# First quad of heads prepared pair by pair, and the software queue's loads in a new order

## The chip, the cores and the metric

One core of one Trainium2 chip runs the whole kernel. The metric is the device time of one execution in microseconds (us); lower is better. Engines are named as in the profile: PE (matrix), PEld (its weight loads), DVE (vector), ACT (scalar), POOL (GpSimd, which also issues the software DMA queue), SP (which issues a hardware DMA queue).

## The reference, cut to what matters

```python
q, k, v: (8, 12, 448, 64)                 # batch, heads, sequence, head width
q_n, k_n = rmsnorm(q, g_q), rmsnorm(k, g_k)
attn = softmax(q_n @ k_n.T / sqrt(64))    # per head, 448 x 448
x = (attn @ v) -> (3584, 768)             # heads side by side again
a, b = x @ w1, x @ w2                     # 768 -> 1024, twice
out = (a * b @ w3) @ w_out                # 1024 -> 1024 -> 768, float32
```

## The kernel before, in words

**Tiling.** The 96 heads are taken in 24 *quads* of four, three quads to a batch. A quad's q and k lie in one buffer as `[128 partitions, q/k, pair x, 7, 64]`: pair x holds two heads, one on each half of the partitions. So the two *pairs* of a quad are x = 0 and x = 1. `w3 @ w_out` does not depend on x, so the kernel forms the product once (`w34s`) in the beginning, from `w3` (transposed on PE into `w3T`) and `w_out`; afterwards each batch costs two products with w1 and w2 (line 868, `xT` with `w1s`/`w2s`), a multiplication, and one product with `w34s`.

**What a quad passes through.** Loads of q and k (line 367); squares on ACT (`sq`, 464); their sums on DVE (`red`, `ssq`, 471); Ln and Exp on ACT for the root (`alpha`, 480 and 483); the multiplication on DVE into bf16 (`scale`, `qks`, 494); a transpose to `[head width, tokens]`, on PE for the first five quads (line 1123, `do_turn`, two turns of seven) and by DMA for the rest (561); copies out of PSUM into `qkT` (352 on ACT, 358 on DVE), where q is also multiplied by the product of the two weight rows (`g_col`); seven *scores* (line 679, four matmuls of 448 columns each), every one followed by an Exp of 128x896 on ACT (701); and then the product with v (*PV*, lines 745 and 766), for two quads at a time mostly. One score takes both pairs: its four matmuls are for u = 0 and u = 1 in each half, and u is the pair:

```python
    for c in range(2):
        ...
        for u in range(2):
            nc.tensor.matmul(
                ...
                lhsT=qkT[u * D : (u + 1) * D, 1, j, cols],
                rhs=qkT[u * D : (u + 1) * D, 0, :, cols],
```

**What sets the order.** The kernel is built by a planner: `Planner.run` walks through time with an estimate for each job (the numbers given to `add`), and writes each engine's instructions in the order in which that plan starts them. On the chip each engine then takes its own list. Constants such as `QUAD`, `HUNGRY`, `PACE`, `STOCK`, `LOW`, `SOON`, `QUIET`, `LATE`, `WARM_TO`, `AHEAD_W3` only move choices in this plan. PE's choices are in `pe_try`: an open PV, scores, *turns* (transposes of `qks` or of w3), and *passes*, a pass being four matmuls of line 868. Where the plan finds nothing for PE before `WARM_TO`, it puts in a filler matmul on zeros (line 1193); sixteen matmuls of 512 columns on zeros (line 1316) stand at the start.

**The loads.** The first quad comes over the two hardware queues, SP and ACT. All weights, v, and q and k of quads 1 to 5 go over the software queue, issued by POOL in the order of `POOL_ORDER`: `wN` is a piece of w3 (512 KB read, 256 KB written as bf16), `oN` a quarter of w_out, `aN` and `bN` thirds of w1 and w2, `qN` q and k of a quad, `vN` its v in four pieces. A pass for `w34s` needs the transposed piece of w3 and the quarter of w_out that it works on; four passes belong to each pair of one `w` and one `o`, 128 in all.

Of the kernel before, what the change touches and what calls it, by code (L numbers as in the profile page):

```python
# [20 lines left out]
SEM = 0.05  # L21
# [3 lines left out]
LAG = {"ACT": 0.11, "DVE": 0.09, "SP": 0.0, "POOL": 0.0}  # L25
AHEAD = {"SP": 2.0, "POOL": 1.6}
AFTER = 0.7
LATE = 0.3
BUSY = 75.0


# [14 lines left out]
class Planner:  # L46
# [11 lines left out]
    def add(self, *args, **kw):  # L58
        self.jobs.append(Job(*args, **kw))
# [136 lines left out]
def kernel(  # L196
# [40 lines left out]
    psum = ctx.enter_context(tc.tile_pool(name="ps", bufs=1, space=PSUM))  # L237

    N_PE_T = 5
    QUAD = 13.0  # L240
    WARM = 15
    WARM_TO = 13.0
    WARM_N = 256
    MAX_PAIRS = 2
    MARGIN = 0.25
    LOW = 2
    PV_BANKS = 6
    HOLD = 0
    SOON = 0
    STARVED = 4  # L250
    HUNGRY = 0.6
    ONE = 0
    PARTS = ((2, 4, 6, 8), (2, 4, 6, 8), (4, 8))
    EARLY_PAIRS = 3
    AHEAD_W3 = 4
    EARLY = 4
    STOCK = 14
    PACE = 1.7
    POOL_ORDER = (
        "o0 w0 w1 w2 o1 o2 o3 q1 v0 w3 w4 q2 w5 a0 v1 w6 w7 v2 a1 v3 q3 a2 b0 b1 q4 q5 b2".split()  # L260
    )
    ON_POOL = (1, 2, 3, 4, 5)
    IN_PARTS = (6, 7, 8)
    FIRST = 3.5
    THIN_FROM, THIN = 8, 2.5
    QUIET = 0.5

    w1s = const.tile([128, CM, DFF], BF, name="w1s")
    w2s = const.tile([128, CM, DFF], BF, name="w2s")
# [80 lines left out]
    def copy_on(engine, out, in_, by=None):  # L350
        if engine == "ACT":
            nc.scalar.activation(  # L352
                out=out, in_=in_, func=AF.Copy, scale=1.0 if by is None else by
            )
        elif by is not None:
            nc.vector.tensor_scalar(out=out, in0=in_, scalar1=by, scalar2=None, op0=MULT)
        else:
            nc.vector.tensor_copy(out=out, in_=in_)  # L358
# [93 lines left out]

    def plan_prep(i):
        s = st[i]
        pe = i < N_PE_T
# [43 lines left out]
        def by_g():  # L501
# [3 lines left out]
                in1=g_b.unsqueeze(1).broadcast_to([NP, 2 * NJ, D]), op=MULT,  # L505
            )

        alpha_at = [INF, INF]
        red_parts = [[], []]
        s["red_at"] = [INF, INF]  # L510
# [135 lines left out]
    def score_ready(t):  # L646
        n = next_score[0]
        if n >= NQ * NU:
            return False
        i, g = divmod(n, NU)  # L650
        if g == 0 and min(p_free(x, i) for x in range(4)) > t:
            return False
        stock = sum(p.name != "w" for p in waiting)
        if stock >= STOCK and t < last_score[0] + PACE:
            return False
        return max(qkT_at[i]) + SEM <= t

    def do_score(t, z):
        n = next_score[0]
# [57 lines left out]
    def pv_size(t):  # L717


        i = next_pv[0]  # L720
        if not pv_one(i, t):
            return 0
        if i + 1 >= NQ:
            return 1
        if pv_one(i + 1, t):
            return 2
        if next_score[0] >= (i + 2) * NU - SOON:
            return 0
        if i == 1:
            return 0  # L730
        stock = sum(p.name != "w" for p in waiting)
        return 1 if stock < LOW or all_of(w34_at, CF) > t else 0

# [376 lines left out]
            tiles = range(NT - 1) if odd else ()  # L1110
        waiting.extend(ffn2_pair(bp, t) for t in tiles)

    turns = [(i, w) for i in range(N_PE_T) for w in range(2)]
    w3_turns = list(range(CF))

    def do_turn(t, i, w, z):
        s = st[i]
        ps = ps_all[:, z, :].bitcast(BF)[:, 0 : NJ * NP].rearrange(
            "p (j s) -> p j s", j=NJ
        )  # L1120
        took = into("t") + NJ * 0.067
        for j in range(NJ):
            nc.tensor.transpose(  # L1123
                ps[:, j], s["qks"][:, w, j].rearrange("p x d -> p (x d)"), ident
            )
        bank_at[z] = INF
        at = t + took + 0.18
        s["sent"][w] = at

        def done(e):  # L1130
            bank_at[z] = e + SEM
            qkT_at[i][w] = e

        add(
            None, {"DVE": 0.53, "ACT": 0.83}, -950.0 + i,
            lambda e: copy_on(e, s["qkT"][:, w], ps, None if w else g_col),
            needs=[lambda: at, lambda: consts_at["g"]], done=done,
        )
        return took
# [28 lines left out]
    def any_turn(t, r, idle, n):  # L1168

        if not idle:  # L1170
            return None
        if turns:
            i, w = turns[0]
            if scaled_at[i][w] <= r:
                turns.pop(0)
                return do_turn(t, i, w, single(idle))
        ready = [fc for fc in w3_turns if w_at["w3"][fc] + SEM <= r]
        if ready and (len(ready) >= n or ready[-1] == CF - 1):
            if ready[0] - len(w34_at) < AHEAD_W3:
                return do_w3_turn(t, w3_turns.pop(0), single(idle))  # L1180
        return None

    def pe_step(t):

        took = pe_try(t, t - MARGIN)
        took = pe_try(t, t) if took is None else took
        if took is None and t < WARM_TO and idle_banks(t):
            return do_warm(single(idle_banks(t)))
        return took
# [108 lines left out]
    with tc.manual_schedule():  # L1298
        nc.vector.memset(warm_t, 0.0)
        nc.vector.memset(eps_t, 64e-6)  # L1300
        nc.vector.memset(ones, 1.0)
        nc.vector.memset(ones[HP:NP, 1], 0.0)
        nc.vector.memset(ones[0:HP, 2], 0.0)
        nc.vector.memset(ones_row, 1.0)
        for which in range(2):
            load_qk(0, which, nc.sync, 0, 1)
            load_qk(0, which, nc.scalar, 1, 2)
        nc.scalar.dma_start(out=g_row[:, 0], in_=g_q.unsqueeze(0))
        nc.scalar.dma_start(out=g_row[:, 1], in_=g_k.unsqueeze(0))
        nc.scalar.preload_act_table_set("natural_log_exp_and_others")  # L1310
        make_identity(nc, ident)
        for t_sb in v_bufs:
            nc.gpsimd.memset(t_sb[:, :, NF, :], 0.0)
        def warm(n):
            for _ in range(n):
                nc.tensor.matmul(  # L1316
                    out=ps_all[:, 7, :], lhsT=warm_t[:, 0:128], rhs=warm_t,
                    start=True, stop=True,
                )

        def g_product():
            nc.vector.scalar_tensor_tensor(
                out=gp_row,
                in0=g_row[:, 0].unsqueeze(1).broadcast_to([1, 2, D]),
                scalar=8.0,
                in1=g_row[:, 1].unsqueeze(1).broadcast_to([1, 2, D]),
                op0=MULT, op1=MULT,
            )
            nc.tensor.matmul(
                out=ps_all[:, 6, 0:D], lhsT=ones_row, rhs=gp_row[:, 0],  # L1330
                start=True, stop=True,
            )
            nc.tensor.matmul(
                out=ps_all[:, 6, D : D + 1],
                lhsT=gp_row.rearrange("a x d -> a (x d)"), rhs=ones_row[:, 0:1],
                start=True, stop=True,
            )
            warm(1)

        def spread():  # L1340
            nc.vector.tensor_copy(out=g_b, in_=ps_all[:, 6, 0:D])
            nc.vector.tensor_copy(out=g_col, in_=ps_all[:, 6, D : D + 1])

        warm(WARM)
        free.update(ACT=4.0, DVE=4.0, SP=4.0, POOL=2.3, PE=7.2)
        plan.now = plan.moved_to = 2.2
        plan.moving["SP"].append([2.3, FIRST, lambda t: None, 0.086])
        landed[0].update(q=4.5, k=5.4)
        bank_at[6] = INF
        add(  # L1350
            "DVE", 0.13, -13.0, g_product, needs=[lambda: 5.8], done=put(consts_at, "gp")
        )
        add(
            "DVE", 0.22, -11.0, spread, needs=[lambda: consts_at["gp"] + 0.6],
            done=lambda t: consts_at.update(g=t + SEM) or bank_at.__setitem__(6, t + SEM),
        )
        for i in range(3):
            plan_prep(i)

        seq = [0]  # L1360

        def weight(emit, moves, done):
            add("POOL", 0.6, -100.0 + seq[0], emit, done=done, moves=moves)

        for name in POOL_ORDER:
            what, x = name[0], int(name[1])
            seq[0] += 1
            if what == "o":
                weight(lambda x=x: load_wout(x), (1.95, 0.135), put(w_at["w_out"], x))
            elif what == "w":  # L1370
                weight(lambda x=x: load_w3(x), (1.27, 0.172), put(w_at["w3"], x))
            elif what == "v":
                plan_load_v(x, -100.0 + seq[0])
            elif what == "q":
                plan_load_qk(x, -100.0 + seq[0])
            else:
                dst, src, key = (w1s, moe_w1, "w1") if what == "a" else (w2s, moe_w2, "w2")
                weight(
                    lambda dst=dst, src=src, x=x: load_w12(dst, src, x), (2.7, 0.323),
                    put(w_at[key], x),  # L1380
                )
        waiting.extend(w34_pair(fc) for fc in range(CF))
        plan.run(pe_step, finished)
        if PLAN_OUT is not None:
            PLAN_OUT.append(dict(free))
# [28 lines left out]
```

## Time and profile before

| what | value |
|---|---|
| median of six runs | 353.68 us (352.86 to 354.38) |
| the profiled execution | 354.06 us, of which 352.2 us are the span from the first to the last instruction |
| granted PE clock over the span | 1.00 |
| busy: PE, ACT, DVE, POOL | 344.6, 262.0, 206.8, 76.8 us |
| DMA, mean over the span | 156 GB/s; 16.92 MB on the software queue |
| first score on PE, first Exp on ACT | 11.29 us, 11.72 us |

Times inside the span count from its start. A row of the timeline or of the chain of work gives start, duration, engine, line, output and input, and how many instructions are merged; a bracket is the idle time of the engine before it and what ended that.

### The profile page before, as it was taken

The numbers are of one execution on the slowest core, as the hardware profiler recorded it, in microseconds if no ns is written. First come the engines' busy times: TensorE is split into PE (matmuls) and PEld (weight loads), VectorE is DVE, ScalarE is ACT, GpSimd is POOL, SyncE is SP. The second block draws the span as 40 slices with busy tenths as digits, with TensorE's granted clock in tenths as the row PEclk, the third lists the DMA queues.
The fourth block names the chain that finished last, engine by engine and source line by source line (L and its number), as shares of the span: only waits on it lengthen the run. The fifth ranks groups of instructions, "written<-read, shape, count | busy, mean of one in ns | idle before, by whom it ended". The sixth has DMA issues, their size and how long they took to land.

```text
span 352.2 us, 16197 instructions
## 1 busy us (share of the span) xinstructions
PE 344.6 (98%) x7374; PEld 225.0 (64%) x7374; DVE 206.8 (59%) x293; ACT 262.0 (74%) x375; POOL 76.8 (22%) x134
## 2 busy tenths in 40 slices
PE   8999999999999999999999999999999999999995
PEld 4767656657655766469856575566665656666674
DVE  5379378997989297895869758566643321222200
ACT  4779979989899989797989898777886942222122
POOL 8376720304212223113131031330130000000000
PEclk9999999999999999999999999999999999999999
DMA  8999999599999999987999979852590013100054
GB/s 194 238 284 192 239 314 238 95 199 235 195 201 187 196 173 227 193 172 176 207 218 166 225 97 254 220 70 40 115 177 6 4 47 105 37 2 2 5 164 153
DMA packets 68488, 55.11 MB, mean 156 GB/s; under 512 B 45060, under 2 KB 62372, under 8 KB 68420
## 3 DMA queue, kind: packets, MB, share of 16 engines
q1 hardware_dynamic: 49440, 35.33, 45.1%
q0 software_dynamic: 18048, 16.92, 27.4%
q10 hardware_dynamic: 932, 1.84, 1.4%
q8 instruction: 57, 0.93, 1.1%
q14 instruction: 11, 0.09, 0.1%
HBM read 46.66 MB, written 11.01 MB: 164 GB/s over the span
## 4 chain that ended last, share of the span: by engine, by line
PE 88%; ACT 5%; DVE 3%; DMA 2%; issue 1%; DVEq 0%; POOLq 0%
PE ps_all L868 62%; PE ps_all L766 11%; PE ps_all L679 9%; ACT P L701 3%; DMA qkT<-qks 2%; PE ps_all L745 2%; PE ps_all L1316 2%; DVE qks L494 1%; PE ps_all L1123 1%; PE ps_all L1064 1%; ACT sq L464 1%; PE ps_all L1145 1%; DVE ssq L471 1%; PE ps_all L1193 1%; DVE xT L808 1%
## 5 line engine op out<-in xcount | busy, mean ns | idle before, releaser
L701 ACT ACTIVATE P<-ps_all 128x896 bf16<-128x896 f32 x114 | 99.4, 922 | 12.3 <-PE ps_all L679 12.0
L407 POOL DMA_DIRECT2D v_sb<-in_v_dram x96 | 57.1, 616 | 177.3 <-PE ps_all L679 89.2
L868 PE MATMUL ps_all<-xT,w2s 64*64 64x448 bf16 x1536 | 88.9, 349 | 0.6 <-DVE xT L808 0.4
L868 PE MATMUL ps_all<-xT,w1s 64*64 64x448 bf16 x1536 | 89.0, 349 | 0.1
L868 PE MATMUL ps_all<-w34s,abT 64*64 64x384 bf16 x1728 | 80.5, 323 | 0.0
L352 ACT ACTIVATE half<-ps_all 128x896 bf16<-128x896 f32 (+1 forms) x38 | 33.3, 877 | 49.4 <-PE ps_all L868 49.3
L949 DVE TENSOR_TENSOR abT<-ps_all,half 128x896 bf16<-128x896 f32 x32 | 34.9, 1089 | 54.4 <-PE ps_all L868 54.3
L868 PEld LDWEIGHTS <-abT 64*64 64x64 bf16 x1728 | 55.1, 107 | 17.3 <-issue 0.7
L868 PEld LDWEIGHTS <-w2s 64*64 64x64 bf16 x1536 | 48.4, 107 | 25.7 <-issue 1.4
L868 PEld LDWEIGHTS <-w1s 64*64 64x64 bf16 x1536 | 47.4, 107 | 25.5 <-POOLq L852 0.9
L679 PE MATMUL ps_all<-qkT 64*64 64x448 bf16 x672 | 62.1, 352 | 0.8 <-ACT Pr L701 0.4
L471 DVE TENSOR_REDUCE ssq<-sq 128x14 f32<-128x896 f32 (+1 forms) x50 | 51.3, 1042 | 18.9 <-ACT sq L464 18.9
L494 DVE TENSOR_TENSOR qks<-qk_sb,al 128x448 bf16<-128x448 f32 x96 | 55.9, 618 | 1.4 <-ACT al L483 1.4
L464 ACT ACTIVATE sq<-qk_sb 128x896 f32<-128x896 f32 (+1 forms) x50 | 45.4, 922 | 1.7 <-DVE ssq L471 1.1
L808 DVE TENSOR_TENSOR xT<-ps_all,r 128x448 bf16<-128x448 f32 x48 | 27.7, 619 | 13.2 <-ACT r L789 10.3
L679 PEld LDWEIGHTS <-qkT 64*64 64x64 bf16 x672 | 23.1, 106 | 14.2 <-issue 4.8
L868 PE MATMUL ps_all<-w_outs,w3T 64*64 64x384 bf16 x512 | 25.1, 323 | 0.7 <-DVE w3T L358 0.5
L701 ACT ACTIVATE w_outs<-ps_all 128x896 bf16<-128x896 f32 x24 | 21.6, 913 | 5.2 <-PE ps_all L679 4.8
L766 PE MATMUL ps_all<-P,v_sb 128*32 128x448 bf16 x456 | 25.2, 353 | 0.0
L766 PEld LDWEIGHTS <-v_sb 128*32 128x32 bf16 x592 | 15.9, 97 | 12.5 <-issue 0.5
L701 ACT ACTIVATE Pr<-ps_all 128x896 bf16<-128x896 f32 x24 | 22.1, 921 | 0.1
L358 DVE COPY half<-ps_all 128x768 f32<-128x768 f32 x13 | 12.4, 955 | 13.9 <-PE ps_all L868 13.2
(65 smaller groups left out, 213.1 us busy)
## 6 DMA issues: line engine op xcount, KB each, us to landing
out_dram<-half SPq DMA_DIRECT2D x48, 192.0 KB, 3.6
qk_sb<-in_q_dram SPq DMA_DIRECT2D x15, 448.0 KB, 5.0
qk_sb<-in_k_dram SPq DMA_DIRECT2D x15, 448.0 KB, 5.6
v_sb<-in_v_dram POOLq DMA_DIRECT2D x48, 64.0 KB, 3.8
v_sb<-in_v_dram POOLq DMA_DIRECT2D x48, 48.0 KB, 3.8
qk_sb<-in_q_dram POOLq DMA_DIRECT2D x5, 448.0 KB, 12.0
qk_sb<-in_k_dram POOLq DMA_DIRECT2D x5, 448.0 KB, 11.8
w3s<-in_moe_w_dram POOLq DMA_DIRECT2D x8, 256.0 KB, 6.7
```

Of the source, the lines that this page charges most:

```text
L352: nc.scalar.activation(out=out, in_=in_, func=AF.Copy, scale=1.0 if by is None else by)
L358: nc.vector.tensor_copy(out=out, in_=in_)
L407: nc.gpsimd.dma_start(out=v_bufs[i % 4][p0 : p0 + HP, g::2, 0 : j1 - j0].rearrange("p h j d -> p h (j d)"), in_=src[:, g::2, j0:j1].rearra ...
L464: nc.scalar.activation(out=s["sq", t][:, x0:x1], in_=src[:, t, x0:x1], func=AF.Square)
L471: nc.vector.tensor_reduce(out=s["ssq"][:, t, x0:x1], in_=s["sq", t][:, x0:x1], axis=AX, op=ADD)
L494: nc.vector.tensor_tensor(out=s["qks"][:, t, :, x], in0=src[:, t, x], in1=s["alpha"][:, t, x].unsqueeze(2).broadcast_to([NP, NJ, D]), op=MULT,
L679: nc.tensor.matmul(out=sc[HP * c : HP * c + HP, u, 0:S].rearrange("p (j s) -> p j s", j=NJ), lhsT=qkT[u * D : (u + 1) * D, 1, j, cols], rh ...
L701: lambda: nc.scalar.activation(out=dst, in_=sc[:, :, 0:S], func=AF.Exp),
L766: nc.tensor.matmul(out=ps_all[hd * HALF : (hd + 1) * HALF, z, 0:S], lhsT=value_weights(i, hd, j, kind), rhs=s["P"][:, hd, j, :] if j < NF ...
L808: lambda: nc.vector.tensor_tensor(out=xT[b][:, 2 * m + kind - 1, :], in0=ps, in1=s["r"], op=MULT),
L868: mm = nc.tensor.matmul(out=ps_all[64 * h : 64 * h + 64, p.bank + z, 0 : p.n], lhsT=lhsT[64 * r : 64 * r + 64, 64 * h : 64 * h + 64], rhs= ...
L949: nc.vector.tensor_tensor(out=abT[bp][:, f0 : f0 + 2, odd * S : (odd + 1) * S], in0=ps_all[:, z : z + 2, 0:S], in1=a_sb[b, f0], op=MULT,)
```

## The change

The first quad no longer goes through `prep`'s general path. `prep_by_pair` takes pair 0 of q and k, then pair 1: squares, sums, one Ln and one Exp for q and k of a pair together, multiplications. `do_pair_turn` transposes 64 columns of `qks` at a time, so a pair of q or k is one turn of seven transposes (four turns instead of two), and copies it to its 64 partitions of `qkT`. The first loads go accordingly: q on SP, k on ACT, pair 0 first on both. `score_ready` lets the plan take the first three scores once pair 0 is there; `do_score` itself is the same. `POOL_ORDER` starts with w0 in place of o0, moves q1 and v0 ahead of w2 and o3, and puts v1, v2 and v3 behind w7, with b0 and a1 before. A number of planner constants change.

```diff
-LATE = 0.3
+LATE = 0.401
-    QUAD = 13.0
+    QUAD = 12.269
-    WARM_TO = 13.0
+    WARM_TO = 12.754
-    MARGIN = 0.25
-    LOW = 2
+    MARGINS = (0.25, 0.0)
+    SINGLES = None
+    BY_PAIR = True
+    LOW = 3
-    SOON = 0
+    SOON = 2
-    HUNGRY = 0.6
+    HUNGRY = 0.609
-    AHEAD_W3 = 4
+    AHEAD_W3 = 6
-    PACE = 1.7
+    PACE = 1.73
     POOL_ORDER = (
-        "o0 w0 w1 w2 o1 o2 o3 q1 v0 w3 w4 q2 w5 a0 v1 w6 w7 v2 a1 v3 q3 a2 b0 b1 q4 q5 b2".split()
+        "w0 o0 o1 w1 o2 q1 v0 w2 o3 w3 w4 q2 w5 a0 w6 b0 a1 w7 v1 v2 v3 q3 b1 a2 q4 q5 b2".split()
     )
-    QUIET = 0.5
+    QUIET = 0.424
+    PAIR_AT = (4.28, 5.36)
...
+    def prep_by_pair(s, src, sq, red, scale):
...
+            for t in range(2):
+                add(
+                    "ACT", 0.40, -14.0 + 2 * x + t * 0.1, lambda t=t: sq(t, x, x + 1),
+                    needs=[lambda: PAIR_AT[x]], done=put(hold[t], "at"),
+                )
+                add(
+                    "DVE", 0.53, -13.0 + 2 * x + t * 0.1, lambda t=t: red(t, x, x + 1),
+                    needs=[lambda t=t: hold[t].get("at", INF) + SEM], done=reduced,
+                )
+                add(
+                    "DVE", 0.54, -16.0 + 2 * x + t * 0.1, lambda t=t: scale(t, x),
+                    needs=[lambda: al.get("at", INF) + SEM], done=done(t),
+                )
+            add(
+                "ACT", 0.45, -16.0 + x, lambda: alpha(x),
+                needs=[lambda: all_of(got, 2) + SEM], done=put(al, "at"),
+            )
...
-        return max(qkT_at[i]) + SEM <= t
+        at = max(pair_at[0]) if BY_PAIR and n < NF else max(qkT_at[i])
+        return at + SEM <= t
...
+    def do_pair_turn(t, x, w, z):
+        s = st[0]
+        rows = slice(D * x, D * x + D)
+        ps = ps_all[:, z, :].bitcast(BF)[rows, 0 : NJ * NP].rearrange(
+            "p (j s) -> p j s", j=NJ
+        )
+        took = into("u") + NJ * 0.067
+        for j in range(NJ):
+            nc.tensor.transpose(ps[:, j], s["qks"][:, w, j, x], ident)
...
+        add(
+            None, {"DVE": 0.53, "ACT": 0.87}, -950.0,
+            lambda e: copy_on(e, s["qkT"][rows, w], ps, None if w else g_col[rows]),
+            needs=[lambda: at, lambda: consts_at["g"]], done=done,
+        )
...
-            load_qk(0, which, nc.sync, 0, 1)
-            load_qk(0, which, nc.scalar, 1, 2)
+            if BY_PAIR:
+                load_qk(0, 0, nc.sync, which, which + 1)
+                load_qk(0, 1, nc.scalar, which, which + 1)
```

## The prediction

> **What bounds it now.** I read the page first, then the timelines of the first 30 us, engine by engine, then the chain of waits, then the windows.
>
> ```profile
> span 352.2 us, 16197 instructions
> PE 344.6 (98%) x7374; PEld 225.0 (64%) x7374; DVE 206.8 (59%) x293; ACT 262.0 (74%) x375; POOL 76.8 (22%) x134
> ```
>
> PE is the bound: 98% busy, and the chain of waits lies on it for 88%. The change takes no useful matmul away. So the end moves by what changes in PE's idle and filler time. The next rows show the start, from the timelines of ACT, DVE and PE.
>
> ```profile
> 4.09 2.23 ACT L464 ACTIVATE sq<-qk_sb 128x448 f32<-128x448 f32 x4 [0.28 <-DMA qk_sb<-in_q_dram]
> ...
> 7.21 2.21 DVE L494 TENSOR_TENSOR qks<-qk_sb,al 128x448 bf16<-128x448 f32 x4
> ...
> 9.01 1.01 ACT L352 ACTIVATE qkT<-ps_all,g_col 128x896 bf16<-128x896 bf16 x1 [1.34 <-PE ps_all L1123]
> ...
> 10.16 0.62 DVE L358 COPY qkT<-ps_all 128x896 bf16<-128x896 bf16 x1 [0.74 <-PE ps_all L1123]
> ...
> 11.72 5.10 ACT L701 ACTIVATE P<-ps_all 128x896 bf16<-128x896 f32 x6 [1.71 <-PE ps_all L679]
> 12.11 0.45 PEld L1145 LDWEIGHTS <-w3s 128*128 128x128 bf16 x8 [0.30 <-DMA w3s<-in_moe_w_dram]
> ```
>
> The chain to the first Exp (11.72) is squares, sums, roots, four multiplications, transposes and copies; PE runs fillers, its first score is at 11.29. The Exps then follow every 0.83 us, and the seventh (16.71) ends at 17.63. The last row shows PE waiting for a piece of w3. POOL's timeline tells when loads land, because from its ninth on, a load waits for the one eight before it:
>
> ```profile
> 10.97 0.60 POOL L407 DMA_DIRECT2D v_sb<-in_v_dram  x1 [0.38 <-DMA w3s<-in_moe_w_dram]
> 12.23 0.59 POOL L407 DMA_DIRECT2D v_sb<-in_v_dram  x1 [0.66 <-DMA w3s<-in_moe_w_dram]
> 14.12 0.59 POOL L407 DMA_DIRECT2D v_sb<-in_v_dram  x1 [1.29 <-DMA w_outs<-in_moe_w_out_dram]
> ...
> 17.99 0.55 POOL L442 DMA_DIRECT2D w3s<-in_moe_w_dram  x1 [1.41 <-DMA w_outs<-in_moe_w_out_dram]
> 19.09 0.72 POOL L367 DMA_DIRECT2D qk_sb<-in_q_dram  x1 [0.56 <-DMA qk_sb<-in_q_dram]
> 20.56 0.73 POOL L367 DMA_DIRECT2D qk_sb<-in_k_dram  x1 [0.75 <-DMA qk_sb<-in_k_dram]
> ```
>
> A piece of w3 takes 1.26 us (10.97 to 12.23), a quarter of w_out 1.89 (12.23 to 14.12), q and k of a quad 1.10 and 1.47. The queue is a belt: an order changes what PE can do when, not the total. Last, quad 1 and the first double PV (DVE, PE, chain of waits):
>
> ```profile
> 20.88 2.07 DVE L471 TENSOR_REDUCE ssq<-sq 128x14 f32<-128x896 f32 x2
> ...
> 27.48 0.36 PE L679 MATMUL ps_all<-qkT 64*64 64x448 bf16 x4
> ```
>
> ```profile
> 45.23 0.69 PE ps_all L745 x24
> ```
>
> **First quad, pair by pair.** Squares and sums keep their count and, as the loads still alternate over two queues, their times; DVE does all four sums before any multiplication. The multiplications move ahead of the two copies of g (7.02 to 7.28), so they start at 7.02 instead of 7.21: four end at 9.23, g at about 9.45. PE now meets the eight transposes of w0 first. POOL's first wake, after o0, is at 8.48; w0 is shorter by 1.89 - 1.26 = 0.63, so the wake comes at 7.85, and PE, which in this trace goes 0.24 ahead of POOL's wake (10.73 against 10.97), starts at 7.6 and ends at 8.2. Seven transposes of half width are not in the trace; a transpose starts every 0.056 to 0.067 us whatever follows, so a turn keeps 0.47. The fourth turn waits for the last multiplication and ends at 10.25. So fourteen more transposes cost 0.94, before PE has other work.
>
> The copies of `qkT` are now four of 64x896, one on ACT behind a `w3T` copy, three on DVE, two of them with the weights. Between half the DVE copy above (0.31) and ACT's weighted one (1.01) I take 0.62: in DVE's own rows, 128 elements on one partition took 0.27 and 64 on 128 partitions 0.20, so partitions don't set it. DVE then copies from 9.45 to 10.07, 10.6 and 11.2; ACT ends its own at 10.3. Since a score reads both pairs, PE's first score waits for 11.2, with passes queued behind it, and the first Exp comes 0.43 later, as before (11.29 to 11.72): 11.65. **Change 0**; bounds -0.6 (three copies at 0.31) to +0.8 (two at 1.01). Scoring pair by pair only happens in the plan.
>
> The Trainium skill ("PSUM — Partial Sum Buffer", section "Engine vs sequencer instructions") says that matmuls start and complete in program order, which speaks against the relaxed test. The trace's own case: at 12.11 the w3 transposes wait 0.30 for their load, and the next pass begins only at 12.67. Were passes free to overtake, 0.33 of the two passes behind the first score would go into the wait.
>
> **Quad 1.** Before its k there now stand two loads less (one w, one o: 1.26 + 1.9 = 3.2), so it is there at 17.4 on POOL's clock instead of 20.56. The Exps of quad 0 end at 17.6, so ACT squares at 17.55 instead of 19.67, and the `w34s` copy that held DVE until 20.88 is gone: the second sum starts at 19.55 instead of 21.87. The rest of the chain has the same instructions in the same order on DVE. First score of quad 1: 27.48 - 2.3 = 25.2.
>
> **What PE has done by then.** From the instruction orders: before, 52 passes of w34s (0.1625 each) and 40 transposes of w3 (0.067); after, 33 and 24. That is 19 x 0.1625 + 16 x 0.067 = **4.16 us of work less, in 2.3 us less time**. The reason is the belt: w2, o3 and with them 24 passes come behind q1 and v0. PE waits for the Exps of quad 0 (it has 22 passes, seven scores and eight transposes, 5.4 us, for 11.2 to about 18.4), then about 1.0 from the end of PV at 20.7 to the turns of quad 1.
>
> **To the double PV.** From 25.2 the order holds 14 scores (2.65), 71 passes (11.5), 40 w3 transposes (2.7) and 14 turns (0.94): 17.8, so 43.1. ACT needs 14 Exps (0.83), two squares (0.89), two roots (0.54), three copies (0.8): 16.9 from 25.6, done at 42.5, just hidden. Before it is 45.23 with all 128 passes done; after, 24 passes (3.9) are left. 43.1 + 3.9 - 45.23 = **+1.8**. w7, v1 to v3 (about 42 by the same belt) and b1, a2 (50) land before they are used; that they come later costs nothing then, and up to 1 if the belt is slower.
>
> **After it.** The scores of quad 3 start at about 55.1 instead of 51.4, since passes left over come before its turns; ACT's list from there to the last Exp of quad 4 took 19.5 (51.95 to 71.44) and holds one square (0.86) less, so it ends at 55.6 + 18.6 = 74.2; PE's own sum (28 turns, 88 passes at 0.189, 14 scores) gives 74.3. With 0.3 of waits as before, the next double PV is at 74.6 instead of 72.78: +1.8 again. From there PE's order is the same as before up to one stretch around quad 15, and the last 57.6 us are passes alone. So the delay stays. The constants QUAD, HUNGRY, PACE, LOW, SOON, LATE and QUIET act through this order only.
>
> **Sum.** 354.06 + 1.8 = 355.9 for the profiled execution, which lay 0.38 above the median of 353.68: **355.5**.
>
> **Rivals.** *The delay is eaten, or more.* Later PE waits for others: the windows show 1.12 us of PE idle in 100 to 150 and 0.48 in 150 to 200, and matmul starts say more, since ends are modelled: 0.81 between two scores at 115.75 (0.19 is normal), 0.78 before 145.81, 0.72 before 153.39, some 3.2 with the small ones. If ACT, DVE and the transposing DMA keep their old times while PE comes 1.8 later, these shrink. From 0.7 eaten it is no change, from 2.9 faster; at 3.2 it is 352.3, with the copies at 0.31 351.7. For it: these waits name ACT, DMA and DVE. Against it: ACT restarts at 77.35, after PE's PV, so it should shift along. Chance 0.26 for faster, 0.18 for the middle (354).
>
> *PE's clock falls.* Fillers of 256 columns drop from 22 to 3. The first nine matmuls of 512 columns start every 0.427 us, from 5.0 on every 0.216. At the slow rate four scores, eight passes and eight transposes around 11 to 14 would take 2.6 more, 1.8 of it in idle time: +0.8, 356.3. With weighted copies at 1.01 besides, 357.1. For it: only transposes run from 7.6 to 10.3. Chance 0.1, within slower.
>
> The Trainium skill's rule ("TensorE: Matmul & The Clock Gate", "What's actually happening" and "Part 4: PE-mode transpose") is a window of about 3.4 us, and it says that transposes don't count as busy. By it the slow rate would come and the time be 356.3. The profile's clock row stays at 9 or more throughout, transposes included, but among fillers.
>
> *It does not do what it says:* that the scores wait for both pairs is in the forecast; had they not, Exps would start at 10.7 (ACT's copy at 10.3, and 0.43), and the sum be +0.9, within 0.3%.
>
> **Numbers.** Slower by over 0.3% (about what a measurement of this kernel can tell from no change) 0.56, of which 0.46 is the forecast itself; within 0.18; faster 0.26. Range 351.7 to 357.1, the ends of the rivals above; the likeliest case alone is 354.9 to 356.3, by the two bounds on the copies.
>
> **What would show it.** Right: first Exp at 11.6, quad 1's first score near 25, double PVs near 43 and 74.6, PE idle before both. Wrong: a first Exp before 11, quad 1's score before 23.5 (the break-even), or less start-to-start waiting at 110 to 155.

## The result, and the profile after

The changed kernel took a median of 355.65 us (354.18 to 357.34, 22 runs), the kernel before, beside it, 354.04 us (352.52 to 355.94, 49 runs). The ratio is **1.0049** (95%: 1.0035 to 1.0063), so the change made the kernel slower by about 1.7 us. A second series gave 1.0035 (1.0014 to 1.0057). The profiled execution of the changed kernel took 356.46 us, 0.8 above its median; its span is 354.7 us. Every time below is of executions near the full granted clock; a single one (598.3 us, granted clock 0.56) is left out.

The page first: PE's busy share is 97% instead of 98%, and its busy time has moved by half a microsecond only. The end has moved, the work has not.

```profile
span 354.7 us, 16184 instructions
PE 345.1 (97%) x7369; PEld 226.4 (64%) x7369; DVE 209.3 (59%) x297; ACT 259.7 (73%) x373; POOL 76.5 (22%) x134
```

Now the start, from the timeline of DVE and then of PE (line numbers are those of the changed kernel: 359 is a copy with the weights on DVE, 361 a plain one, 743 a score, 811 a double PV).

```profile
9.63 1.40 DVE L359 TENSOR_SCALAR qkT<-ps_all,g_col 64x896 bf16<-64x896 bf16 x2
10.95 0.62 DVE L361 COPY qkT<-ps_all 64x896 bf16<-64x896 bf16 x1
```

```profile
10.85 0.37 PE L743 MATMUL ps_all<-qkT 64*64 64x448 bf16 x1
11.62 0.38 PE L743 MATMUL ps_all<-qkT 64*64 64x448 bf16 x3 [0.40 <-DVE qkT L361]
...
25.15 0.38 PE L743 MATMUL ps_all<-qkT 64*64 64x448 bf16 x4
...
43.27 0.38 PE L811 MATMUL ps_all<-Pr,ones 64*32 64x448 bf16 x8
...
75.75 0.38 PE L811 MATMUL ps_all<-Pr,ones 64*32 64x448 bf16 x8
```

The first matmul of the first score, that of pair 0, starts at 10.85. The second, that of pair 1, waits for DVE's last copy, and nothing behind it on PE goes ahead. So the score is complete only after 11.62, and the first Exp follows at 12.05. Quad 1's first score is at 25.15 (27.48 before), the first double PV at 43.27 (45.23), but the next one at 75.75 (72.78). On ACT one sees what came late on the way to it:

```profile
12.05 4.96 ACT L765 ACTIVATE P<-ps_all 128x896 bf16<-128x896 f32 x6 [2.22 <-PE ps_all L743]
...
49.29 0.95 ACT L525 ACTIVATE sq<-qk_sb 128x896 f32<-128x896 f32 x1 [1.47 <-DMA qk_sb<-in_k_dram]
...
55.72 0.95 ACT L525 ACTIVATE sq<-qk_sb 128x896 f32<-128x896 f32 x1 [2.53 <-DMA qk_sb<-in_q_dram]
```

The squares of quads 3 and 4 wait for their loads, 1.47 and 2.53 us. In the stretch before, the chain of work lies on POOL, which issues v, and on its loads; PE joins it at 54.62:

```profile
39.52 1.78 POOL v_sb L410 x4
41.38 0.46 issue
41.84 0.09 POOL v_sb L410
42.01 0.41 issue
42.42 1.02 POOL qk_sb L370 x2
43.44 0.40 issue
43.85 0.15 POOL w2s L439
44.00 0.42 issue
44.42 10.15 DMA w1s<-in_moe_w_dram
54.62 1.33 PE ps_all L934 x24
```

PE's passes with the last third of w1 begin at 54.62, when that third has landed. It was issued at 44.42, after a row of v pieces of which POOL issued the last five one every 0.58 us. The windows of the same stretch show how busy the DMA engines were (the last three columns are the granted clock, the DMA share and GB/s). Before:

```profile
35.00:40.00 5.00, 5.00 (x116) 3.41 (x115) 2.19 (x4) 4.70 (x6) 3.59 (x6) 1.00 1.12 259
40.00:45.00 5.00, 5.00 (x128) 3.53 (x120) 1.81 (x3) 5.00 (x7) 3.00 (x5) 1.00 1.04 216
```

And after:

```profile
35.00:40.00 5.00, 5.00 (x125) 3.68 (x120) 0.70 (x2) 5.00 (x7) 1.67 (x3) 1.00 1.04 154
40.00:45.00 5.00, 5.00 (x124) 2.89 (x116) 2.32 (x3) 2.33 (x4) 5.00 (x10) 1.00 0.78 103
```

The share falls to 0.78 and the rate to 103 GB/s. So two things stand in this trace: the passes left over, which the prediction counted, and a software queue that delivered less, which it did not.

A second trace of the same kernel (354.54 us, the fastest execution of its series) has the first of the two, with 24 passes left at 43.46, but not the waits. Its ACT starts the squares of quads 3 and 4 without waiting for a load, its PE does not wait for w1s, and its double PV is at 75.15:

```profile
47.05 1.77 ACT L525 ACTIVATE sq<-qk_sb 128x896 f32<-128x896 f32 x2
...
53.57 0.95 ACT L525 ACTIVATE sq<-qk_sb 128x896 f32<-128x896 f32 x1
```

```profile
75.15 0.38 PE L811 MATMUL ps_all<-Pr,ones 64*32 64x448 bf16 x8
```

In that trace the loads were earlier before any piece of v1 to v3 came: w7 landed at 37.53, against 39.23 in the first. So the waits above need not come with this order of loads; they were there in an execution whose loads were late besides. The experiments try to take the two things apart.

### The profile page after: what moved, and what is told of

The parts are those of the page before. It is cut to its first block, busy times and chain, and to the rows that moved or that the text cites. A ratio compares the mean times of both kernels' runs of the same rounds, so it can differ in the third digit from the quotient of the medians.

```text
span 354.7 us, 16184 instructions
## 1 busy us (share of the span) xinstructions
PE 345.1 (97%) x7369; PEld 226.4 (64%) x7369; DVE 209.3 (59%) x297; ACT 259.7 (73%) x373; POOL 76.5 (22%) x134
## 4 chain that ended last, share of the span: by engine, by line
PE 74%; DMA 13%; ACT 3%; DVE 3%; POOL 2%; issue 2%; SPq 1%; ACTq 0%; POOLq 0%; DVEq 0%
PE ps_all L934 55%; PE ps_all L832 9%; PE ps_all L743 7%; DMA w1s<-in_moe_w_dram 7%; DMA qk_sb<-in_q_dram 3%; DMA w3s<-in_moe_w_dram 2%; PE ps_all L811 2%; ACT P L765 1%; DMA qk_sb<-in_k_dram 1%; ACT half L355 1%; DVE abT L1015 1%; DVE qks L555 1%; PE ps_all L1130 1%; POOL v_sb L410 1%; SPq L624 1%
## 5 line engine op out<-in xcount | busy, mean ns | idle before, releaser
L934 PEld LDWEIGHTS <-w2s 64*64 64x64 bf16 x1536 | 49.8, 107 | 23.7 <-issue 0.8
L934 PEld LDWEIGHTS <-w1s 64*64 64x64 bf16 x1536 | 48.6, 107 | 25.3 <-issue 1.0
L743 PEld LDWEIGHTS <-qkT 64*64 64x64 bf16 x672 | 24.4, 106 | 16.2 <-issue 6.4
L832 PE MATMUL ps_all<-P,v_sb 128*32 128x448 bf16 x456 | 25.2, 353 | 0.1
```

Source lines behind the costliest of these rows:

```text
L743: nc.tensor.matmul(out=sc[HP * c : HP * c + HP, u, 0:S].rearrange("p (j s) -> p j s", j=NJ), lhsT=qkT[u * D : (u + 1) * D, 1, j, cols], rh ...
L832: nc.tensor.matmul(out=ps_all[hd * HALF : (hd + 1) * HALF, z, 0:S], lhsT=value_weights(i, hd, j, kind), rhs=s["P"][:, hd, j, :] if j < NF ...
L934: mm = nc.tensor.matmul(out=ps_all[64 * h : 64 * h + 64, p.bank + z, 0 : p.n], lhsT=lhsT[64 * r : 64 * r + 64, 64 * h : 64 * h + 64], rhs= ...
```

## The experiments

**The three parts, each alone.** The change has a pair path, an order of loads and a set of constants. Each was put into the kernel before by itself.

Order alone:

```diff
-        "o0 w0 w1 w2 o1 o2 o3 q1 v0 w3 w4 q2 w5 a0 v1 w6 w7 v2 a1 v3 q3 a2 b0 b1 q4 q5 b2".split()
+        "w0 o0 o1 w1 o2 q1 v0 w2 o3 w3 w4 q2 w5 a0 w6 b0 a1 w7 v1 v2 v3 q3 b1 a2 q4 q5 b2".split()
```

> The kernel before with the new order of the software queue alone (no pair path, old constants); from the double PV of quads 3 and 4 on, PE's list is that of before and of after. Theory A (the loss comes from the loads' order, which leaves PE short of passes for the first 40 us): +1.0 to +2.2 us, first double PV near 43 with 24 passes left. Rival B (the loss comes from the pair path: more turns and copies, a first score that waits for both pairs): within 0.4 us of before. Rival C (the constants): within 0.4 us of before.

Pair path alone (the constants and the order of before):

```diff
+    BY_PAIR = True
+    def prep_by_pair(s, src, sq, red, scale):
+    def do_pair_turn(t, x, w, z):
```

> The pair path and the first loads by pair alone, with the old order on the software queue and the old constants; from the fifth quad on PE's list is that of before. Theory A: within 0.5 us of before, since the first Exp comes at 11.7 to 12.2 as in both kernels. Rival B: +1.3 to +2 us, the whole loss. Rival C: within 0.4 us of before.

Constants alone:

```diff
-    QUAD = 13.0
+    QUAD = 12.269
...
-    QUIET = 0.5
+    QUIET = 0.424
```

> The changed planner constants alone. PE's list is that of before up to quad 8. Theory A and rival B: within 0.3 us of before. Rival C: +1.3 to +2 us.

| kernel | median us (runs) | ratio to before (95%) | first score of quad 1 | double PVs | last PV |
|---|---|---|---|---|---|
| before, profile | 354.06 | | 27.48 | 45.2, 72.7 | 283.5 |
| order alone | 355.86 (11) | 1.0051 (1.0032 to 1.0069) | 25.05 | 43.3, 74.9 | 285.6 |
| pair path alone | 355.53 (12) | 1.0034 (1.0018 to 1.0049) | 28.89 | 46.3, 73.8 | 284.1 |
| constants alone | 354.33 (10) | 0.9989 (0.997 to 1.0009) | 28.39 | 46.1, 73.6 | 283.4 |
| all three (after) | 355.65 (22) | 1.0049 (1.0035 to 1.0063) | 25.15 | 43.3, 75.8 | 285.8 |

The order alone costs as much as the whole change. The constants show no cost. Their row shows one thing more: up to 185 us PE's order there is that of before, and yet its PVs lie 0.9 us later at 46.1 and 73.6, because the loads came 1.0 later in that execution (POOL's wake for quad 1's k at 21.58 against 20.56). By 147.7 that is gone (147.6 before). So 0.9 us of lateness in the first third is made up again.

The pair path alone was not expected to cost anything. Its profiled execution was the fastest of the twelve (354.56 us), so its trace need not show the whole 1.2 us. ACT's timeline of that run shows a place in its order:

```profile
19.16 0.95 ACT L525 ACTIVATE sq<-qk_sb 128x896 f32<-128x896 f32 x1 [1.50 <-DMA qk_sb<-in_q_dram]
21.60 0.81 ACT L355 ACTIVATE w34s<-ps_all 128x768 bf16<-128x768 f32 x1 [1.48 <-PE ps_all L934]
22.31 0.94 ACT L525 ACTIVATE sq<-qk_sb 128x896 f32<-128x896 f32 x1
```

The plan put a copy of `w34s` between the two squares of quad 1. The copy waits 1.48 for passes on PE, so the second square starts at 22.31 although k landed at 20.74. Quad 1's first score comes 8.2 us behind that landing, where it was 7.2 in before (20.27 to 27.48) and 7.1 in the run of the constants. In after both squares stand together, at 17.65. That this place alone makes the 1.2 us was not shown; a second run with the pair path and the old order, now with the new constants, was meant to test it:

```diff
-        "w0 o0 o1 w1 o2 q1 v0 w2 o3 w3 w4 q2 w5 a0 w6 b0 a1 w7 v1 v2 v3 q3 b1 a2 q4 q5 b2".split()
+        "o0 w0 w1 w2 o1 o2 o3 q1 v0 w3 w4 q2 w5 a0 v1 w6 w7 v2 a1 v3 q3 a2 b0 b1 q4 q5 b2".split()
```

> The kernel after with before's order of the loads: the pair path and the new constants, without the new order. In the run with the pair path alone, ACT's order had a copy of w34s between the two squares of quad 1, and the copy waited for passes, so that the second square began 1.5 us later than its k allowed and quad 1's first score came about 1 us late. Here ACT's order has no copy between those squares. Theory A (the pair path by itself costs nothing; that place in ACT's order was the +0.34%): first score of quad 1 about 7.2 us behind the landing of its k, as in before, and not 8.2; ratio to before 0.9985 to 1.0015. Rival (the price is in the pair path itself: the blocked first score, the half-width turns, the copies of 64 rows): 1.0025 to 1.0045 again.

It was the opposite: 357.62 us, ratio 1.0116 (1.0069 to 1.0162). The expectation was mistaken in its premise: ACT's order there does have the copy between the squares, at 21.98, and the second square follows at 22.69; quad 1's first score came at 29.28, 8.6 behind its k. But its plan also differs from that of before at other places, so the rest of the 1.16% can't be put down to one step. What the pair path costs with the old order stays open.

**More passes early.** If the missing passes are the cost, w2 and o3 ahead of q1 and v0 should help.

```diff
-        "w0 o0 o1 w1 o2 q1 v0 w2 o3 w3 w4 q2 ...
+        "w0 o0 o1 w1 o2 w2 o3 q1 v0 w3 w4 q2 ...
```

> The changed kernel with w2 and o3 put back ahead of q1 and v0 on the software queue; PE has 48 passes again before the first PV instead of 24 (the planner's later order differs too). Theory A: 1.0 to 1.8 us of the 1.6 come back (354.0 to 354.7 against 354.0 before). Rival B: it stays at +1.3 to +2 us.

A miss: 357.27 us, 1.0085 (1.006 to 1.0109). The first double PV came at 44.4 with 16 passes left, the next at 76.6. This kernel kept the run of v1, v2 and v3, and its ACT waited 1.16 and 1.70 us for q and k of quad 4. PE's order also differs from that of after from 18 us on. Either can hide what the edit was meant to show, so no run puts back the missing passes alone.

**The run of v alone.** That led to the loads. From the trace's landing times, the pieces of v1 to v3 took 1.16, 1.39 and 1.37 us in before, in three groups of four, 3.9 in all, and the load behind the last group landed 1.0 later. In after they are one run of twelve: 5.1 us (39.23 to 44.31), and the load behind it lands 2.5 later. In the run with the order alone it was 5.9, in that with w2 and o3 put back 5.5. Over all twelve traces that can be compared, the twelve pieces and the load behind them took 7.2 to 8.0 us where they are one run (six traces) and 4.5 to 5.5 where they are three groups (six traces). To test it without touching the plan, the order in which POOL issues the loads was written apart from the order that the planner counts with. All engines but POOL keep their instructions and their order. First, the kernel before with such a run:

```diff
-        ... q2 w5 a0 v1 w6 w7 v2 a1 v3 q3 a2 b0 b1 q4 q5 b2
+        ... q2 w5 w6 w7 a0 a1 v1 v2 v3 q3 a2 b0 b1 q4 q5 b2     (issued; the plan as before)
```

> The kernel before, with its plan and every engine's order kept, and only POOL's order of loads changed from w5 a0 v1 w6 w7 v2 a1 v3 q3 to w5 w6 w7 a0 a1 v1 v2 v3 q3: the same loads up to q3, but the pieces of v1 to v3 in one run of twelve. Theory A: the run takes over 5 us where the three groups took 3.9 together, the load behind it lands about 1 late too, and q3 to q4 land 2 to 3 us later than in before; the double PV of quads 3 and 4 comes 0.5 to 1.2 later, the time is 0.3 to 1.1 us longer: ratio 1.001 to 1.003. Rival B (the queue takes its total whatever the order, as the prediction said): q3 to q4 land within 1 us of before and the ratio is within 0.001 of 1.

355.86 us against 354.01, ratio **1.0046** (1.0024 to 1.0068): more than expected, and as much as the whole change. POOL's timeline, then PE's:

```profile
37.13 2.96 POOL L410 DMA_DIRECT2D v_sb<-in_v_dram  x5 [1.82 <-DMA w1s<-in_moe_w_dram]
40.05 0.78 POOL L368 DMA_DIRECT2D qk_sb<-in_q_dram  x1
```

```profile
47.63 0.38 PE L748 MATMUL ps_all<-Pr,v_sb 64*32 64x448 bf16 x8 [1.07 <-ACT w34s L353]
...
59.08 0.38 PE L682 MATMUL ps_all<-qkT 64*64 64x448 bf16 x4 [1.22 <-ACT P L704]
...
76.37 0.38 PE L748 MATMUL ps_all<-Pr,ones 64*32 64x448 bf16 x8
```

The last five pieces are issued without a wait, 0.59 us each, while a piece in a group took 0.2 to 0.8 on the queue, mostly under 0.5. The run takes 5.95 us (36.85 to 42.80), and q of quad 4 lands at 57.3 instead of 52.5. ACT stands in front of the squares of quads 3 and 4 for 1.21 and 1.42 us, with copies and Exps queued behind, and PE waits for these: 1.07 and 1.22 in the rows. The double PV is at 76.4 instead of 72.7, the last PV at 286.2. Of these 3.7 us some 0.5 need not be the run's: this execution was already that late at its first PV (22.56 against 22.06), ahead of every load that was moved. The loads w6, w7, a0 and a1 move a little with the run; in this trace neither PE nor ACT waits for one of them. The rival (the queue takes its total whatever the order) has fallen.

Why the run takes longer is argued, not shown. POOL's issuing can be only a part of it: between two pieces issued 0.59 apart, at 37.13 and 37.72, the landings lie 2.72 apart (39.43 and 42.15). From 39.5 to 42.2 the DMA share was 0.89, so the engines were busy, but at 107 GB/s; from 42.2 to 44.5, with the long loads behind the run, 0.94 at 358 GB/s. After's first trace has both: a share of 0.35 from 40 to 41, then 0.96 at 101 GB/s to 42.5. So a rival, that small pieces move slowly when no long load moves beside them, was not tested apart.

Then the reverse, the kernel after without the run:

```diff
-        ... q2 w5 a0 w6 b0 a1 w7 v1 v2 v3 q3 b1 a2 q4 q5 b2
+        ... q2 w5 w6 a0 v1 w7 b0 v2 a1 v3 q3 b1 a2 q4 q5 b2     (issued; the plan as after)
```

> The kernel after, with its plan and so every engine's order kept, and only the order in which POOL issues the loads changed: w6 ahead of a0, v1 behind a0, v2 behind b0, a1 behind v2, v3 behind a1. So the twelve pieces of v1 to v3 are no longer one run but three groups of four with a long load between them, as in before. Theory A (the run of twelve small loads dries the software queue, since POOL needs 0.58 us to issue a piece that takes 0.2 to 0.4 on the queue; q3, a2 and q4 come about 3 us later for it, and the double PV of quads 3 and 4 about 1.1 us later): q of quad 4 lands at 52 to 54 instead of 55.7, PE no longer waits for w1s near 54, that double PV starts at 74.4 to 75.0 instead of 75.75, and the time is 0.4 to 1.1 us under that of after: ratio to before 1.002 to 1.004. Rival B (later waits eat whatever is won at 75): that anchor moves, the end does not: 1.0049 as after. Rival C (a0, b0 and a1, which now come later, are missed): over 1.0055.

355.67 us, ratio 1.0039 (1.0018 to 1.006). The trace is that of another execution:

> The same kernel as f7_v_apart, for its trace at the full granted clock. Theory A: with v1 to v3 in three groups PE does not wait for w1s near 54, and the double PV of quads 3 and 4 starts 1.8 us later than in before (72.8 to 73.6 in the two profiles of its plan), so at 74.4 to 75.0 and not at 75.75; q of quad 4 lands near 51. Rival B: that PV stays at 75.5 or later although q of quad 4 is early, since PE's order alone sets it.

```profile
43.14 0.38 PE L814 MATMUL ps_all<-Pr,ones 64*32 64x448 bf16 x8
...
74.60 0.38 PE L814 MATMUL ps_all<-Pr,ones 64*32 64x448 bf16 x8
```

With the groups apart the waits for q, k and w1s near 49 to 56 are gone, q of quad 4 lands at 50.65, and the two double PVs stand at 43.14 and 74.60, where the prediction had 43.1 and 74.6. Against after's first trace that is 1.15 us less at the second. How much of it is the run of v, and whether it reaches the end, was asked once more, with after beside it on one chip:

> The kernel after, unchanged, timed on the same chip as the next kernel. Both theories: ratio to before 1.0035 to 1.0063, as in the first result.

> The kernel after with v1 to v3 in three groups of four, as in f7_v_apart, whose trace had the double PV of quads 3 and 4 at 74.6 and its last PV 1.7 us earlier than after's, while its timed ratio was 1.0039 with an interval that also holds 1.0049. Theory A (the run of twelve small loads is part of after's loss to the end): its median is 0.4 to 1.5 us under that of h1_after. Rival B (later waits eat it): within 0.3 us of it.

After: 355.85 us, 1.0035 (1.0014 to 1.0057). With the groups apart: 355.36 us, 1.0040 (1.0012 to 1.0069). The medians and the ratios point different ways, and no difference is resolved. In the trace of after the run took 6.5 us (37.53 to 44.04), and q of quad 4 landed at 53.55; in that with the groups apart it landed at 51.09. But in neither does PE or ACT wait for these loads, and the second double PV is at 75.15 in the one and 74.89 in the other, the last PV at 283.9 and 284.7. So in this pair of traces the run makes 0.3 us at 75, and no loss at the end. Of the 1.15 us above, 0.60 and 0.29 are differences between two executions of the same kernel. With the groups apart 1.0039 and 1.0040 are left, about 1.4 us (0.6 to 2.1 by the first interval). That this is the price of the missing passes agrees with the 24 passes left in each of these traces, but it is found by taking away the rest.

The two costs do not seem to add: without the run 1.4 us, the run alone (in the kernel before) 1.6 us, both together 1.2 to 1.8. A likely reason is that PE, when it is already late by the passes, needs the late loads only when they have landed. The second trace of after and that of the order alone speak for it: both have the run, and from 44 to 62 us neither PE nor ACT waits for a load. It is an argument from these traces and not a run of its own.

**The plan that counts with both pairs.** `do_score` needs both pairs, the plan counted with one.

```diff
-        at = max(pair_at[0]) if BY_PAIR and n < NF else max(qkT_at[i])
+        at = max(max(pair_at[0]), max(pair_at[1])) if BY_PAIR and n < NF else max(qkT_at[i])
```

> The kernel after, whose plan now lets the scores of quad 0 start only when both pairs are turned and copied, as they do on the chip: passes and transposes stand ahead of the first score in PE's order instead of behind it. Theory A (the first score that stood blocked for 0.59 us cost PE only that, at a time when it had work to spare): first score no longer blocked, first Exp 12.0 to 12.4, ratio to before within 0.0015 of after's: 1.0035 to 1.0065. Rival (planning with a time at which the score can't start upset the order of passes behind it and is part of the loss): the first double PV comes 0.5 us or more earlier than 43.3 with the same 24 passes left, ratio 1.003 or less.

356.76 us, 1.006 (1.0036 to 1.0084). The first score starts at 11.71 and is not blocked; the first Exp is at 12.15, the double PVs at 43.4 and 75.3. So taking the block away gained nothing, as expected. That PE did later, while it would have waited for the Exps anyway, what it could not do behind the block, is the likely reason; it was not shown.

None of these kernels beats the one before by more than the measurement can tell.

## Why the prediction was right, and where its steps failed

**The start.** The first Exp was put at 11.65 and came at 12.05 (before 11.72). The mis-sized term is the row of copies on DVE: it took 1.94 us (9.63 to 11.57; 0.68 for a copy with the weights, not 0.62) instead of 1.75, and it began at 9.63, not 9.45. The rest held: three copies in a row on DVE, the first score waiting for the last of them, the Exp 0.43 behind it. Pair by pair the scores run only in the plan.

**Quad 1.** Predicted 25.2, measured 25.15; 25.05 with the order alone. Its k was on POOL's clock at 17.96 instead of 17.4, the squares at 17.65 instead of 17.55.

**The first double PV.** Predicted 43.1 with 24 passes left (its terms add up to 43.0); measured 43.27 and 43.46 with 24 passes behind it, and 43.14 and 43.26 with the groups of v apart. This was the core of the forecast. At the end the kernels with the groups apart lose 1.4 us where the sum had 1.8.

**The next one.** Predicted 74.6; 75.75 in after's first trace, 75.15 in its second, 74.60 and 74.89 with the groups apart. The step that failed is the sentence that the queue is a belt, on which "an order changes what PE can do when, not the total": the run and the load behind it took 7.2 to 8.0 us instead of 4.5 to 5.5. The prediction priced the loads singly and put v1 to v3 "about 42 by the same belt", a2 and b1 at 50; they landed at 44.3, 54.6 and 52.1 in the first trace, at 44.0, 52.5 and 49.9 in the second. It allowed up to 1 us for a slower belt. After's second double PV came 1.15 and 0.55 us behind the forecast, with the groups apart 0.0 and 0.3, so the run's part is 0.3 to 1.15, and the executions' own late loads are in it. A row that hints at it was there: POOL's issues of v at 22.38 in the trace of before, four in 2.44 us, against the 1.16 that these four took on the queue.

The Trainium skill ("DMA: Bandwidth & Descriptors", section "Anatomy of one DMA — SWDGE (gpsimd) path") gives one such load a fixed cost of about 2.0 us besides its bytes. After's first trace comes near it where little else was queued: the last piece of the run, 48 KB, was issued at 41.84 and landed at 44.31, 2.47 us later. In its second trace the same piece took 3.89 us, so it is not the whole of it.

**"So the delay stays."** Half right. Against before's profile, after's PVs are 3.0 us late from 75.8 to 126, 2.2 at 150, 1.2 at 197 to 219, and 2.3 at the end; in its second trace 2.4 at 75.15 and 0.4 at the end. So the later waits, which the first rival named, take up 0.7 us in the one and 2.0 in the other, and 0.9 in the run of the constants. The prediction argued against it that ACT restarts behind PE's PV and shifts along; that was too strong. That 355.5 was met within 0.2 is in part luck: the queue's extra and what is made up later have opposite signs, and neither was in the sum.

**The rivals.** "The delay is eaten, or more" did not come true in the median: the waits took up a part only. "PE's clock falls" did not come either: after 3.0 us with transposes and one filler only (7.08 to 10.07) the two passes start 0.19 apart and the fillers 0.12, where the slow rate of the first matmuls (0.427 for 512 columns) would give 0.32 and 0.21. The Trainium skill's window of 3.4 us ("TensorE: Matmul & The Clock Gate", section "What's actually happening") was not filled, so this run doesn't test its rule on transposes. Nor would the prediction's own stretch, 7.6 to 10.3, have filled it, so that by the window the slow rate was not due.

**The pair path.** It was costed at nothing. With the new order nothing speaks against that: order alone and all three together have the same ratio. With the old order it cost 0.34%, and 1.16% with the new constants besides; that was not foreseen, and its cause is open.

## What to carry to other kernels

Do not price an order of loads by the sum of single loads: twelve small ones in a row, with the load behind them, took the queue 7.6 us here on average, and 4.9 in groups between long loads. Compare the time to issue one with the time that it takes on the queue, and keep long loads between them. Take a second trace of the same kernel before a wait is put down to an edit: here the waits of the first were not in the second. A load that is moved forward takes other work's place: count what the bound engine has left to do at the next fixed point, not when the moved data arrive. And where a planner writes the order, an edit in one place can move another engine's list; comparing every engine's list, and keeping the plan while only the loads are permuted, tells the two apart.

## What the runs showed of the hardware that was not expected

- Half the partitions did not make DVE's copies out of PSUM cheaper: the plain one took 0.62 for 64x896 and for 128x896, the one with the weights 0.68 for both. (ACT's took 0.91 for 64x896 without the weights and 1.01 for 128x896 with them, which is no like pair.)
- Twelve small loads in one run took 5.1 to 6.5 us on the software queue, in groups of four between long loads 3.5 to 4.3.
- The same kernel's loads landed up to 2.1 us apart in two executions (the last third of w1 at 54.57 and 52.45), and its last PV was at 285.8 in one trace and at 283.9 in the other. One trace does not settle an end to better than 2 us; the two double PVs of these traces lie 0.2 and 0.6 apart.
